# A linear-attention, gated-MLP and mixture-of-experts kernel: a first activation placed ahead, and fewer unread matmuls

## The chip, the cores and the metric

The kernel runs on one core of a Trainium2 chip. The metric is the device time of one execution in microseconds, as the median of several runs. The core's engines work side by side and meet at semaphores: TensorE (PE) multiplies matrices, VectorE (DVE) and ScalarE (ACT) do elementwise work, GpSimd (POOL) does fills, some elementwise work and indexed transfers, and SyncE (SP) issues the other transfers. Each engine takes its instructions in order.

## The reference, cut to what matters

```python
# 1. linear attention: batch 4, 8 heads, 768 tokens, head size 48
f = 1.0 / (1.0 + np.exp(-f_logit))
for t in range(S):
    state = f[:, :, t, :, None] * state + np.einsum('bhd,bhe->bhde', k[:, :, t], v[:, :, t])
    y[:, :, t] = np.einsum('bhd,bhde->bhe', q[:, :, t], state)
# 2. gated MLP on 3072 tokens x 384, with 1536 hidden columns; x is y with its heads side by side
gate = 1.0 / (1.0 + np.exp(-(x @ w_gate)))
x = gate * (x @ w_val) @ w_out
# 3. top-1 mixture of 8 experts with 1024 hidden columns
expert_idx = np.argmax(x @ w_gate2, axis=1)          # its softmax weight is gate_w
out[i] = gate_w[i] * (np.maximum(x[i] @ w1[e], 0) @ w2[e])   # e = expert_idx[i], if it has room
```

The weights of part 2 arrive in 64 bits per number and are turned into 32-bit numbers on the chip.

## The kernel before, in words

The 3072 tokens are 24 tiles of 128. The first six tiles (SPLIT_FROM) go through attention in one form, the later ones in another; only the first form bears on the change. Its stages for tile i are: s0a transposes the forget logits on TensorE (line 372) and takes Tanh of half of them on ScalarE (line 386); s0b makes the decay of it (Identity, line 397), a sum for a range check (Exp, line 399) and a running product over the tokens by a scan on VectorE (line 405, result ck); s0c takes a reciprocal (414) and a second scan (416, result cq); s1 transposes k and q on TensorE (441, 443); s1b multiplies them by ck and cq on VectorE (458, results kt and qt); s3 transposes kt back (509); s2 makes the scores (482) and s2b masks them on VectorE (501); s4 makes the state (542); s5 the output (626); s6 transposes it (647) for the MLP.

Beside it the 36 pieces of the MLP's weights are converted, one piece per call of weights_step: three bit operations on VectorE (784, 792, 799) make 32-bit numbers, ScalarE (866) and VectorE (867) split them into a high and a low part. For a piece of w_out TensorE also transposes it (862), ScalarE copies that (873), and TensorE multiplies it by the gate of part 3 (884), whose result VectorE splits (891, 892).

From about 48 us the MLP runs over 8 blocks of three tiles: line 904 makes gate and value, lines 914 to 922 combine them, line 937 multiplies by w_out. Attention of later tiles and conversion of later pieces run between its matmuls. The experts follow from line 1295 on.

The string EARLY (lines 29 to 35) lists the stages of the first tiles and the conversions (W) ahead of the MLP. Between them stand calls of pace: it issues matmuls of a constant tile, pace_in, whose result no instruction reads, and keeps them in program order. PACE has three numbers: how many stand at the very start, how many right behind the first transposes of tile 0, and how many behind each W and each stage that uses TensorE. The list has 34 places of the last kind, so PACE = (7, 12, 2) makes 7 + 12 + 68 = 87.

Within the kernel's text a scheduler orders the instructions of TensorE, VectorE, ScalarE and GpSimd by its own estimates of when their inputs are ready; SyncE's queue keeps the order of the text (manual_schedule). So a change in a few instructions can move others. The first loads are issued in the order of the string LOADS: the forget logits of tile 0, then k and q of tile 0 (k0), a piece of raw weights (r0), the logits of tile 1 (f1), and so on; q of tile 1 is the second transfer of k1.

```python
LOADS = "k0 r0 f1 r1 v0 k1 r2 r3 v1"
PACE = (7, 12, 2)
```

```python
            if i == 0:
                pace(PACE[1])
```

```python
            if item == "W":
                weights_step()
                pace(PACE[2])
```

Of the kernel before, what the change touches and what calls it, by code (L numbers as in the profile page):

```python
# [14 lines left out]
AF = mybir.ActivationFunctionType  # L15
# [36 lines left out]

PIECE = 192

PACE = (7, 12, 2)

DECAY_ON_POOL = 6
X_MIN = -80.0
# [12 lines left out]
def kernel(  # L71
# [15 lines left out]
    nc = tc.nc  # L87
# [69 lines left out]
    def by_head(t):  # L157
        return t.rearrange("p (h d) -> p h d", h=H)
# [56 lines left out]
    z_all = const.tile([P, NTILE], F32, name="z_all")  # L215
    tiny = const.tile([P, 2], F32, name="tiny")
# [4 lines left out]
    def select(t, fill, pattern, base, cmul, op=ALU.is_ge):  # L221
        nc.gpsimd.affine_select(
            out=t, in_=t, pattern=pattern, compare_op=op, fill=fill, base=base, channel_multiplier=cmul
        )

    def make_constants():
        nc.gpsimd.memset(ident, 0.0)
        select(ident, 1.0, [[-1, P]], 0, 1, ALU.not_equal)
        for t, pad in ((xf_r, X_PAD), (xq_r, 0.0), (xk_r, 0.0)):
            for z in range(2):  # L230
                nc.gpsimd.memset(by_head(t[:, z])[:, :, D:], pad)
        nc.gpsimd.memset(decay[:, ::PS], 0.0)
        nc.gpsimd.memset(lim, DECAY_CLAMP)
        nc.gpsimd.memset(flush[:, 0:1], 512.0)
        nc.gpsimd.memset(flush[:, 1:2], -512.0)
        nc.gpsimd.memset(one, 1.0)
        nc.gpsimd.memset(tiny[:, 0:1], -(2.0**-15))
        nc.gpsimd.memset(tiny[:, 1:2], 2.0**-15)
        nc.gpsimd.memset(below, 0.0)
        nc.gpsimd.memset(half, 0.5)  # L240
        nc.gpsimd.memset(mask, 1.0)
        select(mask, 0.0, [[1, P]], 0, -1)
        for z in range(2):
            r = slice(HT * z, HT * z + HT)
            nc.gpsimd.tensor_copy(hmask[r], mask[r, r])
        nc.gpsimd.memset(e_all, 1.0)

        nc.gpsimd.memset(umask, 1.0)
        select(umask[:, 0:D], 0.0, [[0, D]], D - 1, -1)
        select(umask[:, D:], 0.0, [[0, D]], -64, 1)  # L250
        select(umask[:, D:], 0.0, [[0, D]], 64 + D - 1, -1)
# [69 lines left out]
    def pace(n):  # L321
        for _ in range(n):
            ins = nc.tensor.matmul(pace_out, lhsT=pace_in[:, 0:P], rhs=pace_in, start=True, stop=True)  # L323
            tc.keep_in_program_order(ins)
# [43 lines left out]
    def s0a(i):  # L368
        if i < SPLIT_FROM:
# [3 lines left out]
            if i == 0:  # L373
                pace(PACE[1])
        else:
# [1010 lines left out]
    with tc.manual_schedule(engines={mybir.EngineType.SP}):  # L1386
        load_f(0)
        nc.vector.memset(pace_in, 1.0)
        pace(PACE[0])
        make_constants()  # L1390
        nc.sync.dma_start(out=wg2, in_=moe2_w_gate.rearrange("(k p) e -> p k e", p=P))
        for what in LOADS.split():
            {"f": load_f, "k": load_qk, "v": load_v, "r": load_raw}[what[0]](int(what[1:]))
# [3 lines left out]
        def weights_step():  # L1397
            n = next_split[0]
            for lag, fn in (
                (2, split3),  # L1400
                (0, convert1),
                (1, split2),
                (0, convert2),
                (0, convert3),
                (1, split2b),
            ):
                if 0 <= n - lag < NU:
                    fn(order[n - lag])
            next_split[0] += 1
# [49 lines left out]
        for item in EARLY.split():  # L1459
# [3 lines that stand above are left out]
            else:  # L1463
                i, stage = item.split(".")
                stages[stage](int(i))
                if stage in ("s0a", "s1", "s2", "s3", "s4", "s5", "s6"):
                    pace(PACE[2])
        started[0] = True
# [375 lines left out]
```

## Time and profile before

| | us |
|---|---|
| median of 3 runs | 860.74 (860.14 to 861.27) |
| profiled execution | 860.37 |
| its span, first to last instruction | 858.6 |

| engine | busy us | share of the span |
|---|---|---|
| TensorE | 838.5 | 98% |
| VectorE | 541.7 | 63% |
| ScalarE | 396.5 | 46% |
| GpSimd | 160.7 | 19% |

Busy time counts the lengths of an engine's instructions without counting a moment twice. An instruction often starts while the one before it is still ending, so what one costs in a row of its like is the distance of their starts, which is a little less than its length. [...]

### The profile page before, as it was taken

The page shows a single profiled execution, that of the slowest core. Times are in us where ns is not written, and L with a number is a line of the kernel's source. Part 1 is how long each engine was busy: PE and PEld are TensorE (multiplying, and loading weights), DVE is VectorE, ACT ScalarE, POOL GpSimd, SP SyncE. Part 2 cuts the span into 40 slices and gives each one's busy share as a digit, 9 for nine tenths or more (in the row PEclk, how much of TensorE's full clock was granted, in tenths as well). Part 3 has the DMA queues.
Part 4 walks back from the last instruction along what each step waited for, and adds up shares of the span by engine and source line. Part 5 has one row for each costly group of instructions (what it writes and reads, how often), then busy time and mean ns, then how long its engine had stood idle before and what let it go on. Part 6 is the DMA issues. An engine that isn't in the chain of part 4 may idle for free.

```text
span 858.6 us, 18219 instructions
## 1 busy us (share of the span) xinstructions
PE 838.5 (98%) x7042; PEld 791.4 (92%) x7042; DVE 541.7 (63%) x1300; ACT 396.5 (46%) x1011; POOL 160.7 (19%) x240
## 2 busy tenths in 40 slices
PE   8999999999999999999999999999899999999995
PEld 5789989999999999999999999999899999999994
DVE  6998988767766766866866763552953544553521
ACT  3543433555455555555555544332642533553421
POOL 2031200001011011110011000110563524432311
PEclk9999999999999999999999999999999999999998
DMA  9955443544653643644444532140665325434000
GB/s 203 208 153 146 140 118 103 116 116 114 147 116 89 170 108 90 168 101 107 130 107 99 134 85 59 47 166 1 206 229 171 134 88 189 163 100 134 27 23 26
DMA packets 137746, 103.74 MB, mean 121 GB/s; under 512 B 66456, under 2 KB 130760, under 8 KB 137650
## 3 DMA queue, kind: packets, MB, share of 16 engines
q1 hardware_dynamic: 134034, 93.04, 40.7%
q0 software_dynamic: 3616, 9.44, 3.3%
q8 instruction: 57, 0.93, 0.5%
q14 instruction: 39, 0.32, 0.1%
HBM read 89.95 MB, written 13.46 MB: 120 GB/s over the span
## 4 chain that ended last, share of the span: by engine, by line
PE 79%; DVE 8%; issue 6%; ACT 3%; DMA 2%; POOL 1%; SPq 0%; POOLq 0%; ACTq 0%; DVEq 0%
PE pg L904 16%; PE acc L937 16%; PE pv L904 16%; PE acc L1316 6%; PE pg L1295 5%; PE pv L1295 5%; PE acc L1331 2%; PE a L681 1%; PE a L525 1%; PE a L470 1%; DMA x<-xt 1%; PE a L1274 1%; PE acc L323 1%; POOL out_dram L1373 1%; PE a L1331 1%
## 5 line engine op out<-in xcount | busy, mean ns | idle before, releaser
L916 DVE SCALAR_TENSOR_TENSOR th<-th,pv 128x384 f32<-128x384 f32 x96 | 52.9, 551 | 86.7 <-PE pv L904 85.5
L904 PE MATMUL pg<-xh,wh 128*128 128x384 f32 x288 | 102.5, 356 | 1.4 <-ACT th L914 1.2
L937 PE MATMUL acc<-oh,hh 128*128 128x392 f32 x288 | 100.5, 349 | 0.0
L937 PE MATMUL acc<-ol,hh 128*128 128x392 f32 x288 | 98.5, 342 | 0.0
L937 PE MATMUL acc<-oh,hl 128*128 128x392 f32 x288 | 98.3, 341 | 0.0
L904 PE MATMUL pg<-xl,wh 128*128 128x384 f32 x288 | 97.2, 337 | 0.3 <-DVE xl L734 0.3
L904 PE MATMUL pg<-xh,wl 128*128 128x384 f32 x288 | 96.8, 336 | 0.0
L904 PE MATMUL pv<-xh,wh 128*128 128x384 f32 x288 | 96.5, 335 | 0.3 <-DVE th L916 0.3
L904 PE MATMUL pv<-xl,wh 128*128 128x384 f32 x288 | 96.6, 335 | 0.0
L904 PE MATMUL pv<-xh,wl 128*128 128x384 f32 x288 | 96.5, 335 | 0.0
L914 ACT ACTIVATE th<-pg 128x384 f32<-128x384 f32 x96 | 46.9, 488 | 99.8 <-PE pg L904 98.3
L921 ACT CAST hh<-th 128x384 fp32r<-128x384 f32 x96 | 49.2, 512 | 87.4 <-DVE th L916 87.4
L922 DVE TENSOR_TENSOR hl<-th,hh 128x384 fp32r<-128x384 f32 x96 | 53.3, 555 | 33.2 <-ACT hh L921 32.7
L821 ACT ACTIVATE piece<-piece,tiny 128x192 f32<-128x192 f32 x144 | 67.1, 467 | 7.0 <-DMA piece<-in_moe_w_out_dram 2.3
L904 PEld LDWEIGHTS pg<-xh,wh 128*128 128x128 f32 x288 | 54.1, 188 | 5.1 <-ACT th L914 2.0
L904 PEld LDWEIGHTS pg<-xl,wh 128*128 128x128 f32 x288 | 54.2, 188 | 0.8 <-DVE xl L734 0.8
L904 PEld LDWEIGHTS pv<-xh,wh 128*128 128x128 f32 x288 | 54.1, 188 | 0.6 <-DVE th L916 0.6
L937 PEld LDWEIGHTS acc<-oh,hh 128*128 128x128 f32 x288 | 54.0, 188 | 0.6
L937 PEld LDWEIGHTS acc<-oh,hl 128*128 128x128 f32 x288 | 54.1, 188 | 0.2
L904 PEld LDWEIGHTS pg<-xh,wl 128*128 128x128 f32 x288 | 54.1, 188 | 0.1
L937 PEld LDWEIGHTS acc<-ol,hh 128*128 128x128 f32 x288 | 54.2, 188 | 0.0
L904 PEld LDWEIGHTS pv<-xl,wh 128*128 128x128 f32 x288 | 54.1, 188 | 0.0
(341 smaller groups left out, 2014.7 us busy)
## 6 DMA issues: line engine op xcount, KB each, us to landing
r<-in_moe_w_dram SPq DMA_DIRECT2D x16, 1536.0 KB, 7.8
raw<-in_moe_w_out_dram SPq DMA_DIRECT2D x12, 384.0 KB, 4.2
raw<-in_moe_w_gate_dram SPq DMA_DIRECT2D x12, 384.0 KB, 3.6
v<-in_v_dram SPq DMA_DIRECT2D x24, 192.0 KB, 3.3
raw<-in_moe_w_val_dram SPq DMA_DIRECT2D x12, 384.0 KB, 3.4
x1d<-x SPq DMA_DIRECT2D x24, 192.0 KB, 1.9
piece<-in_moe_w_gate_dram SPq DMA_DIRECT2D x24, 192.0 KB, 3.6
piece<-in_moe_w_val_dram SPq DMA_DIRECT2D x24, 192.0 KB, 3.4
```

The costliest lines, as they stand in the source:

```text
L323: ins = nc.tensor.matmul(pace_out, lhsT=pace_in[:, 0:P], rhs=pace_in, start=True, stop=True)
L470: nc.tensor.matmul(sc[z][t, p * HT : (p + 1) * HT], lhsT=pair(kt, p)[64 * z : 64 * z + D, t], rhs=pair(qt, p)[64 * z : 64 * z + D, t], sta ...
L821: nc.scalar.activation(out=words[:, :, 0], in_=words[:, :, 1], func=AF.Sign, bias=tiny[:, z : z + 1], accum_out=above[:, z, n % NF : n % N ...
L904: nc.tensor.matmul(ps[:, 0:nt], lhsT=w[:, kk, :], rhs=x[:, kk, 0:nt], start=(m == 0), stop=(m == len(ops) - 1))
L914: nc.scalar.activation(out=th[:, 0:nt], in_=pg[:, 0:nt], func=AF.Tanh, scale=0.5)
L916: nc.vector.scalar_tensor_tensor(out=g[:, 0:nt], in0=th[:, 0:nt], scalar=1.0, in1=pv[:, 0:nt], op0=ALU.add, op1=ALU.mult)
L921: nc.scalar.copy(out=hh[:, 0:nt], in_=g[:, 0:nt])
L922: nc.vector.tensor_tensor(out=hl[:, 0:nt], in0=g[:, 0:nt], in1=hh[:, 0:nt], op=ALU.subtract)
L937: nc.tensor.matmul(acc[i][:, 0:DE], lhsT=a[:, ts], rhs=w, start=(f == 0 and m == 0), stop=(f == NF - 1 and m == 2),)
L1295: nc.tensor.matmul(ps, lhsT=wt[:, kk, fs], rhs=x[:, kk, c0 : c0 + w], start=(m == 0), stop=(m == len(ops) - 1))
L1316: nc.tensor.matmul(acc[e, d][:, 0 : CAPS[e]], lhsT=w[:, f, d * P : (d + 1) * P], rhs=a[:, 0 : CAPS[e]], start=(f == 0 and m == 0), stop=(f ...
L1331: nc.tensor.matmul(acc[e, j][0:n, 0:DM], lhsT=a[:, ss], rhs=w[:, f], start=(f == 0 and m == 0), stop=(f == NF2 - 1 and m == 2),)
```

## The change

Two places are edited. The middle and last numbers of PACE are halved. And behind make_constants, which fills the constants on GpSimd, a Tanh of one column is added on ScalarE: it reads the constant tiny and writes the first column of z_all, a column that the sum of tile 0 (line 399) overwrites later. Lines behind 1390 move down by one.

```diff
--- before.py
+++ after.py
@@ -52,7 +52,7 @@
 
 PIECE = 192
 
-PACE = (7, 12, 2)
+PACE = (7, 6, 1)
 
 DECAY_ON_POOL = 6
 X_MIN = -80.0
@@ -1388,6 +1388,7 @@
         nc.vector.memset(pace_in, 1.0)
         pace(PACE[0])
         make_constants()
+        nc.scalar.activation(out=z_all[:, 0:1], in_=tiny[:, 0:1], func=AF.Tanh)
         nc.sync.dma_start(out=wg2, in_=moe2_w_gate.rearrange("(k p) e -> p k e", p=P))
         for what in LOADS.split():
             {"f": load_f, "k": load_qk, "v": load_v, "r": load_raw}[what[0]](int(what[1:]))
```

SyncE's and GpSimd's orders stay as they were. TensorE's, VectorE's and ScalarE's differ up to about 95 us and agree from there on. A number behind a name is a buffer's.

ScalarE, before, its first instructions (decay is the Tanh of tile 0's logits, a_183 the logits transposed):

```order
L386 ACT_TABLE_LOAD [waits PE_49]
L386 ACTIVATE decay<-a_183 128x4x128 [waits Pool_49]
L397 ACTIVATE decay<-decay,bias 128x4x128 [waits Activation_49,Pool_49]
L399 ACTIVATE a_183,z_all<-a_183 128x512
L386 ACTIVATE decay<-pv 128x4x128 [waits DVE_49,PE_49,Activation_49]
```

And after (a_184 is the same tile as a_183):

```order
L1391 ACT_TABLE_LOAD
L1391 ACTIVATE z_all<-tiny 128x1 [waits Pool_49]
L386 ACTIVATE decay<-a_184 128x4x128 [waits PE_49]
L397 ACTIVATE decay<-decay,bias 128x4x128 [waits Activation_49,Pool_49]
L399 ACTIVATE a_184,z_all<-a_184 128x512
L386 ACTIVATE decay<-pv 128x4x128 [waits DVE_49,PE_49,Activation_49]
```

The table load stands first now, with no wait, and the new instruction behind it waits for GpSimd. The rows behind are as they were but for kn, the copy of line 511, which comes earlier.

TensorE, before, from the transposes of kt of tile 0 (a_251) to its scores (a_260, a_261):

```order
L509 MATMUL a_251<-ident,kt 128x112 [waits DVE_49]
L509 MATMUL a_251<-ident,kt 128x112 x3
L323 LDWEIGHTS pace_in
L323 MATMUL acc_124<-pace_in 128x512
L323 LDWEIGHTS pace_in
L323 MATMUL acc_124<-pace_in 128x512
L482 MATMUL a_260<-qt,kt 128x128 [waits DVE_49,Activation_49]
L482 MATMUL a_261<-qt,kt 128x128 [waits PE_49]
L482 MATMUL a_260<-qt,kt 128x128
```

And after, from the transposes of kt (a_242) to the scores (a_250, a_251); acc_278 is q of tile 1:

```order
L509 MATMUL a_242<-ident,kt 128x112 [waits DVE_49]
L509 MATMUL a_242<-ident,kt 128x112 x3
L323 LDWEIGHTS pace_in
L323 MATMUL acc_124<-pace_in 128x512
L443 MATMUL acc_278<-ident,xq 128x128 [waits DMAHW1_49,PE_49]
L443 MATMUL acc_278<-ident,xq 128x128 x2
L482 MATMUL a_250<-qt,kt 128x128 [waits DVE_49,Activation_49]
L482 MATMUL a_251<-qt,kt 128x128 [waits PE_49]
L482 MATMUL a_250<-qt,kt 128x128
```

One filler stands in place of two at each place, and three of the four transposes of tile 1's q, which wait for a load (DMAHW1), have come in front of the scores.

VectorE, before, from the second scan of tile 1 to the split of the first w_out piece's last columns (oh_274; a_337 and a_339 are the masked scores of tile 0, kt and qt are tile 1's):

```order
L416 SCALAR_TENSOR_TENSOR cq<-decay,lim 128x516
L867 TENSOR_TENSOR ol_275<-a,oh_274 128x384
L867 TENSOR_TENSOR wl_326<-a,wh_325 128x384
L501 TENSOR_TENSOR a_337<-a_260,mask 128x512
L784 TENSOR_SCALAR a<-raw 128x384
L501 TENSOR_TENSOR a_339<-a_261,mask 128x512
L792 SCALAR_TENSOR_TENSOR a<-raw,a 128x384
L458 TENSOR_TENSOR kt<-pv,ck 128x512
L799 SCALAR_TENSOR_TENSOR a<-raw,a 128x384
L891 CAST oh_274<-acc_317 128x8
L458 TENSOR_TENSOR qt<-acc_290,cq 128x512
L892 TENSOR_TENSOR ol_275<-acc_317,oh_274 128x8
```

And after, from the first bit operation on the third piece to the products of tile 1 (oh_263 is the same tile as oh_274):

```order
L784 TENSOR_SCALAR a<-raw 128x384
L416 SCALAR_TENSOR_TENSOR cq<-decay,lim 128x516
L867 TENSOR_TENSOR wl_312<-a,wh_311 128x384
L891 CAST oh_263<-acc_303 128x8
L792 SCALAR_TENSOR_TENSOR a<-raw,a 128x384
L892 TENSOR_TENSOR ol_264<-acc_303,oh_263 128x8
L799 SCALAR_TENSOR_TENSOR a<-raw,a 128x384
L501 TENSOR_TENSOR a_322<-a_250,mask 128x512
L501 TENSOR_TENSOR a_324<-a_251,mask 128x512
L458 TENSOR_TENSOR kt<-pv,ck 128x512
L458 TENSOR_TENSOR qt<-acc_278,cq 128x512
```

The split of line 891 has come forward: the two masked scores, the product kt, and the bit operations 792 and 799 of the third piece stand behind it now.

## Rows read from the trace of the kernel before

**Rows 1.** The page: busy time of each engine, then the chain that ended last by engine

```profile
PE 838.5 (98%) x7042; PEld 791.4 (92%) x7042; DVE 541.7 (63%) x1300; ACT 396.5 (46%) x1011; POOL 160.7 (19%) x240
...
PE 79%; DVE 8%; issue 6%; ACT 3%; DMA 2%; POOL 1%; SPq 0%; POOLq 0%; ACTq 0%; DVEq 0%
```

**Rows 2.** Busy us (instructions) of PE, PEld, DVE, ACT, POOL; clock, DMA share, GB/s

```profile
5.35:48.20 42.85, 41.38 (x337) 29.93 (x336) 38.54 (x86) 21.58 (x46) 4.75 (x13) 1.00 1.02 217
...
10.00:24.00 14.00, 12.88 (x116) 9.39 (x115) 13.93 (x30) 5.58 (x13) 0.19 (x1) 1.00 1.00 211
...
34.00:52.40 18.40, 18.29 (x140) 14.04 (x137) 17.31 (x41) 8.72 (x19) 6.83 (x16) 1.00 0.93 203
...
140.00:848.00 708.00, 704.17 (x6079) 675.98 (x6077) 421.75 (x1038) 336.36 (x887) 134.22 (x154) 1.00 0.41 115
```

**Rows 3.** ScalarE in order of time: start, length, line, operation, [idle before]

```profile
5.64 1.28 ACT L386 ACT_TABLE_LOAD   x1 [5.64 <-PE a L372]
6.93 0.60 ACT L386 ACTIVATE decay<-a 128x512 f32<-128x512 f32 x1
7.62 0.72 ACT L397 ACTIVATE decay<-decay,bias 128x512 f32<-128x512 f32 x1
```

**Rows 4.** VectorE in order of time, the same columns

```profile
8.38 1.23 DVE L405 TENSOR_TENSOR_SCAN ck<-decay,lim 128x516 f32<-128x516 f32 x1 [5.52 <-ACT decay L397]
...
20.09 0.69 DVE L458 TENSOR_TENSOR kt<-pv,ck 128x512 f32<-128x512 f32 x1
20.69 0.55 DVE L799 SCALAR_TENSOR_TENSOR a<-raw,a 128x384 uint32<-128x384 uint32 x1
21.16 0.16 DVE L891 CAST oh<-acc 128x8 fp32r<-128x8 f32 x1
...
41.78 0.56 DVE L867 TENSOR_TENSOR ol<-a,oh 128x384 fp32r<-128x384 f32 x1 [0.39 <-ACT oh L866]
...
42.52 0.17 DVE L891 CAST oh<-acc 128x8 fp32r<-128x8 f32 x1 [0.17 <-PE acc L884]
...
47.18 0.17 DVE L891 CAST oh<-acc 128x8 fp32r<-128x8 f32 x1 [0.41 <-PE acc L884]
```

**Rows 5.** TensorE in order of time, the same columns

```profile
1.53 3.17 PE L323 MATMUL acc<-pace_in 128*128 128x512 bf16 x7 [1.53 <-DVE pace_in L1388]
...
5.35 3.23 PE L323 MATMUL acc<-pace_in 128*128 128x512 bf16 x14
...
10.59 0.59 PE L323 MATMUL acc<-pace_in 128*128 128x512 bf16 x2
...
12.28 0.60 PE L509 MATMUL a<-ident,kt 112*128 112x112 f32 x4 [1.10 <-DVE kt L458]
...
13.25 1.16 PE L482 MATMUL a<-qt,kt 48*128 48x128 f32 x16
...
14.79 0.49 PE L862 MATMUL pg<-ident,a 128*128 128x128 f32 x3
...
15.54 0.60 PE L441 MATMUL pv<-ident,xk 128*128 128x128 f32 x4
...
16.94 0.67 PE L542 MATMUL a<-v,kn 128*64 128x48 f32 x16
...
17.98 0.73 PE L884 MATMUL acc<-wg,wot 128*128 128x8 f32 x6
```

**Rows 6.** SyncE's queue: the load of the second tile's q

```profile
8.05 1.85 SPq L287 DMA_DIRECT2D xq<-in_q_dram  x1
```

**Rows 7.** Transfers issued from 8.0 to 8.5: KB each, us to landing

```profile
xq<-in_q_dram SPq DMA_DIRECT2D x1, 192.0 KB, 5.3
```

**Rows 8.** The matmuls of line 323: ns min/median/max, first and last start

```profile
L323 PE MATMUL acc<-pace_in x87: 376/379/634, 1.5 to 48.0; 128*128 128x512 bf16 x87
```

**Rows 9.** TensorE's last matmul

```profile
847.76 0.34 PE L1331 MATMUL acc<-w2h,hl 128*112 128x384 f32 x1
```

**Rows 10.** Busy time by stretch at the end, columns as in group 2

```profile
852.00:852.50 0.50, 0.00 (x0) 0.00 (x0) 0.00 (x0) 0.00 (x0) 0.00 (x0) 0.50 0.20 29
```

## The prediction

> **What bounds the kernel now.** I read the page first, then busy time by stretch, the engines' rows in order of time for the first 50 us, the landing times, and the end of the span. TensorE is busy for 98% of the span and has 79% of the chain of waits [rows 1]. From 140 to 848 us it is busy for 704.17 of 708.00 us [rows 2]. There is next to no idle time in which to win back or lose anything, so whatever lead the start hands over at about 140 us reaches the end unchanged. The change lies in the first 48 us only, and there the picture differs. Of TensorE's time in that stretch a large part is the filler of line 323, whose results nobody reads: 87 matmuls in all, the last at 48.0 us [rows 8]. What is full there is VectorE: 13.93 of 14.00 us from 10 to 24 us and 17.31 of 18.40 from 34 to 52.4 us [rows 2]. So the start is a race of two full engines, and only one of them is full of work that must be done. The head of it is one chain: filler, four transposes of tile 0's forget logits, ScalarE's table load of 1.28 us, Tanh at 6.93 us, the Identity at 7.62 us [rows 3], and VectorE's first scan at 8.38 us, after 5.52 us of waiting [rows 4].
>
> **The table load.** In the order before, the load carries the wait for the transposes; after, it stands first on ScalarE with no wait, and the one-column Tanh behind it waits for POOL alone. ScalarE is idle for its first 5.64 us [rows 3], so both fit ahead of the transposes. Tanh can then start at 5.64 instead of 6.93 us: 1.28 us off the head, and VectorE's first scan moves from 8.38 to 7.10 us. The added instruction costs nothing, as ScalarE has nothing else then; were POOL's constant later than the transposes, the gain would shrink by that lateness. Bounds: 0 to 1.28 us, taken as 1.28. [...]
>
> **The filler.** A filler matmul costs (3.23 - 0.59) / 12 = 0.22 us on TensorE at the full clock: 14 of them last 3.23 us and 2 of them 0.59 us [rows 5]. Of 87, 7 + 6 + 34 x 1 = 47 stay, so 40 go: 40 x 0.22 = 8.8 us of TensorE's time. If TensorE were the bound throughout, all 8.8 us would be won; if VectorE were, nothing. VectorE's rows are the nearer: from 10 to 24 us it is idle for only 0.07 us, so there nothing can be won behind the head. From 34 to 52.4 us it is idle for 1.09 us, of which three waits make 0.39 + 0.17 + 0.41 = 0.97 us. Two are for line 884 on TensorE and one is for ScalarE's copy, which stands in the same queue of conversions [rows 4]. With half the filler TensorE gets to line 884 earlier, and I count these 0.97 us as won (bounds 0 and 1.09).
>
> **What the new order costs.** The scheduler moves the real work too, and SyncE's queue is unmoved. After, TensorE has three transposes of the second tile's q (line 443) in front of the scores of the first tile (line 482). That q is issued at 8.05 us [rows 6] and lands 5.3 us later [rows 7], at 13.35 us, and no change makes it earlier: its issue waits for no engine. TensorE's queue is in order, so the scores, line 862, line 542 and line 884 wait behind it. Before, line 482 started at 13.25 and line 884 at 17.98 us, 4.73 us apart, with 8 fillers and four line-443 transposes between [rows 5]. After, 4 fillers (0.88 us) and three transposes (0.45 us, at 0.60 for four by line 441) are gone from between, and the three stand in front: 13.35 + 0.45 + 4.73 - 0.88 - 0.45 = 17.20 us, and line 884 ends 0.73 us later, at 17.93 us.
>
> VectorE needs that result for line 891. Before, line 891 came 21.16 - 8.38 = 12.78 us after the first scan, all of it dense. After, five of the instructions stand behind it instead of in front: two of line 501, one kt product (0.60 us from start to start; the mask products of the same size taken like it), one of line 792 and one of line 799 (0.47 us, the one taken like the other) [rows 4]. They are 3 x 0.60 + 2 x 0.47 = 2.74 us. VectorE is there at 7.10 + 12.78 - 2.74 = 17.14 us and waits until 17.93: a new wait of 0.79 us that eats over half of the head start. The same line comes a second time, near 29 us, early in the new order, behind a cut-up line 626. Its wait lies between 0 and 0.79 us; I take 0.30, nearer to 0, since by then the loads come sooner too.
>
> **Sum.** 1.28 - 0.79 - 0.30 + 0.97 = 1.16 us. The profiled execution took 860.37 us (858.6 of span and 1.8 around it), so it would take 859.21. It lies 0.37 us under the median of the runs, 860.74, so the median would be 859.58, said as 859.6. A measurement of this kernel can tell about 0.2%, 1.7 us, from no change; so the forecast is a small gain that counts as none.
>
> **Rivals.** *The new waits don't come.* If q lands earlier, or VectorE is later than my sum, both new waits vanish: 1.28 + 0.97 = 2.25 us, 858.5; with every idle moment of VectorE up to 52.4 us gone it is 2.4 us, 858.3, and more only if later waits go too. For it: VectorE was never idle from 10 to 24 us, whatever TensorE did. Against it: the landing is a row, and TensorE's order is fixed.
>
> *The clock falls in the new gap; slower.* After, kt is ready no sooner than 7.10 + 1.23 + 0.69 = 9.02 us (scan and product [rows 4], with the short reciprocal between them left out), line 509 lasts 0.60, one filler 0.22, and TensorE then has nothing from 9.84 until 13.35: up to 3.5 us idle, where before the longest gap near there was 1.10 us [rows 5], at a granted clock of 1.00 all through [rows 2]. [...] If the clock falls, TensorE's work from 13.35 to 17.93 us, 4.58 us, doubles at worst, and VectorE waits for it: 1.28 - (0.79 + 4.58) - 0.30 + 0.97 = -3.42, 864.2. If the clock is back after half of that work, it is -1.13, 861.9. I take the middle, 863.0. It decides once more than 1.16 us is lost to the half clock. Against it: at the front 7 fillers run at half speed, in 3.17 us, and the 14 behind them in 3.23 us [rows 5], so the clock came back soon once TensorE was kept busy.
>
> *The clock stays down until the dense matmuls.* It may be the filler that holds the full clock between the small matmuls and transposes of the start, and half of it may not do. TensorE is busy for 41.38 us from 5.35 to 48.20 us [rows 2], of which 80 x 0.22 = 17.6 are filler and 23.8 the rest. With 40 fillers, 8.8 us, it is 32.6 us, at half clock 65.2, or 22 us more than the 42.85 us of that stretch: about 883. [...]
>
> *The change doesn't do what it says*: hardly, as the order shows the load ahead and 40 fillers gone.
>
> **How the numbers follow.** Forecast 0.46, 859.6 with its own range 858.4 to 860.9. No new waits 0.27, 858.5, reaching to 857.2. Clock falls in the gap 0.21, 863.0, from 861.7 to 864.2. Clock stays down 0.04, 883. The rest, 0.02, slower. Faster by over 0.2% means below 859.0: 0.08 of the forecast's share and 0.25 of the second, 0.33. Slower means above 862.5: 0.15 of the third, with the last two, 0.21. Within 0.2% is the rest, 0.46. The range 857.3 to 863.6 leaves out a little of the second case below, and above it the worst of the third and all of the fourth.
>
> **What would show it.** Tanh of tile 0 at 5.6 us and the first scan at 7.1 (table load). TensorE idle from about 10 to 13.4 us with line 443 behind it, and VectorE waiting 0.8 us for line 884 ahead of its first line 891 near 17 to 18 us (new wait). No waits of VectorE for line 884 near the old 42.5 and 47.2 us (filler). A granted clock of 1.00 from 10 to 48 us (no rival three or four). From 140 us on every row should stand earlier by one and the same amount, the gain. I am wrong if that amount is over 1.7 us, if the clock falls, or if the stretches from 52 to 140 us, where the order also differs a little, change it by more than 1 us.

## The result, and the profile after

The changed kernel takes 870.23 us (median, 868.42 to 870.81), and the kernel before took 860.44 us (859.94 to 861.27) beside it: a ratio of 1.0113 [1.01, 1.0127], or 9.8 us slower. The forecast was 859.6 us in a range of 857.3 to 863.6, with a chance of 0.21 for slower. It was wrong in sign, and the miss of 10.6 us is nine times its sum of 1.16. The profiled execution took 870.42 us, with a span of 868.7.

The busy times of the page hardly differ from those of [rows 1]: TensorE has 1.7 us more in spite of 40 fewer matmuls, and its share of the chain rose from 79 to 84%.

```profile
PE 840.2 (97%) x7002; PEld 795.2 (92%) x7002; DVE 542.8 (62%) x1300; ACT 396.8 (46%) x1012; POOL 160.2 (18%) x240
...
PE 84%; issue 5%; DVE 4%; ACT 2%; DMA 2%; POOL 1%; SPq 1%; POOLq 0%; DVEq 0%; ACTq 0%
```

Busy time by stretch, in the columns of [rows 2], with the clock ahead of the last two:

```profile
5.00:11.00 6.00, 4.36 (x28) 2.61 (x26) 4.41 (x9) 3.09 (x7) 0.80 (x16) 1.00 1.15 239
11.50:18.00 6.50, 4.43 (x25) 3.46 (x26) 3.24 (x8) 1.31 (x4) 0.43 (x1) 0.50 1.20 262
18.50:24.50 6.00, 4.79 (x49) 3.84 (x47) 5.20 (x12) 2.60 (x7) 0.00 (x0) 1.00 0.59 151
25.00:31.50 6.50, 6.50 (x45) 4.41 (x43) 4.82 (x10) 2.17 (x6) 0.19 (x1) 0.50 0.97 175
32.00:38.00 6.00, 5.00 (x42) 4.48 (x41) 4.23 (x13) 1.77 (x4) 0.00 (x0) 1.00 0.22 56
39.00:45.00 6.00, 5.90 (x30) 4.19 (x31) 4.88 (x12) 1.82 (x4) 0.00 (x0) 0.50 0.75 158
46.00:59.00 13.00, 10.69 (x87) 8.91 (x87) 11.94 (x28) 5.92 (x14) 6.66 (x16) 1.00 0.71 174
59.50:62.00 2.50, 2.50 (x10) 2.40 (x9) 1.72 (x6) 0.84 (x2) 0.00 (x0) 0.50 0.49 105
63.00:848.00 785.00, 778.81 (x6610) 746.32 (x6609) 495.34 (x1198) 370.43 (x957) 144.86 (x169) 1.00 0.42 118
```

The clock, TensorE's granted one as a share of full speed, which [rows 2] show at 1.00 throughout, falls to 0.50 four times before 63 us and not again until the end. By the records of the clock the four falls last 23.9 us together. The row from 25.0 to 31.5 us also shows why busy time misleads: TensorE is "busy" all of it, with 45 matmuls at a clock of 0.50. And VectorE, full in [rows 2], has holes now: 3.24 of 6.50, 4.82 of 6.50, 4.88 of 6.00.

ScalarE's head, answering [rows 3] (start, length, line, operation, [idle before]):

```profile
0.81 1.28 ACT L1391 ACT_TABLE_LOAD   x1 [0.81 <-PEq L1827]
2.91 0.20 ACT L1391 ACTIVATE z_all<-tiny 128x1 f32<-128x1 f32 x1 [0.81 <-POOL tiny L237]
5.11 0.60 ACT L386 ACTIVATE decay<-a 128x512 f32<-128x512 f32 x1 [2.00 <-PE a L372]
```

Then VectorE, answering [rows 4]:

```profile
6.56 1.23 DVE L405 TENSOR_TENSOR_SCAN ck<-decay,lim 128x516 f32<-128x516 f32 x1 [3.69 <-ACT decay L397]
...
17.67 0.36 DVE L784 TENSOR_SCALAR a<-raw 128x384 uint32<-128x384 uint32 x1 [3.26 <-PE pg L862]
...
20.42 0.17 DVE L891 CAST oh<-acc 128x8 fp32r<-128x8 f32 x1 [0.80 <-PE acc L884]
...
27.94 0.69 DVE L501 TENSOR_TENSOR a<-acc,mask 128x512 f32<-128x512 f32 x1 [1.47 <-PE pv L482]
...
32.28 0.17 DVE L891 CAST oh<-acc 128x8 fp32r<-128x8 f32 x1 [1.00 <-PE acc L884]
...
35.21 0.17 DVE L891 CAST oh<-acc 128x8 fp32r<-128x8 f32 x1 [1.38 <-PE acc L884]
...
43.64 0.69 DVE L501 TENSOR_TENSOR a<-a,mask 128x512 f32<-128x512 f32 x1 [1.12 <-PE a L482]
...
47.96 0.56 DVE L867 TENSOR_TENSOR ol<-a,oh 128x384 fp32r<-128x384 f32 x1 [0.82 <-ACT oh L866]
...
49.99 0.16 DVE L891 CAST oh<-acc 128x8 fp32r<-128x8 f32 x1
...
55.00 0.15 DVE L891 CAST oh<-acc 128x8 fp32r<-128x8 f32 x1
```

And TensorE, answering [rows 5] and [rows 9]:

```profile
9.98 0.38 PE L323 MATMUL acc<-pace_in 128*128 128x512 bf16 x1
13.57 0.88 PE L443 MATMUL acc<-ident,xq 128*128 128x128 f32 x3 [3.21 <-DMA xq<-in_q_dram]
14.37 2.08 PE L482 MATMUL a<-qt,kt 48*128 48x128 f32 x16
...
16.79 0.85 PE L862 MATMUL pg<-ident,a 128*128 128x128 f32 x3
...
19.65 0.73 PE L884 MATMUL acc<-wg,wot 128*128 128x8 f32 x6
...
54.36 0.44 PE L904 MATMUL pg<-xh,wh 128*128 128x384 f32 x1
...
57.57 0.44 PE L904 MATMUL pg<-xl,wh 128*128 128x384 f32 x1 [2.15 <-DVE xl L657]
...
857.36 0.34 PE L1331 MATMUL acc<-w2h,hl 128*112 128x384 f32 x1
```

The first scan starts 1.82 us earlier (8.38 to 6.56). TensorE then stands still for 3.21 us until q lands, and the clock falls in that time, at 11.3 us. The sixteen scores take 2.08 us where they took 1.16, and VectorE waits 3.26 us for line 862. The last matmul ends up 9.60 us later (847.76 to 857.36). The loss is made at the start. Before, the first line 904 was this:

```profile
48.48 0.44 PE L904 MATMUL pg<-xh,wh 128*128 128x384 f32 x1
```

It comes 5.88 us later now, and the tenth matmul of its name 9.95 us later (68.29 to 78.24). Between these two TensorE took 19.8 us before and takes 23.9 now. In this stretch lie the wait of 2.15 us for line 657 on VectorE, where TensorE waited 0.28 us at most before, and the last fall of the clock. The first matmul of the experts whose rows are x2h, line 1295, comes 9.5 us later (639.7 to 649.2). TensorE, at full clock from 63 us on, carries the loss to the end.

### The profile page after: what moved, and what is told of

It is laid out like the page before. It is cut to its first block, busy times and chain, and to the rows that moved or that the text cites. A ratio compares the mean times of both kernels' runs of the same rounds, so it can differ in the third digit from the quotient of the medians.

```text
span 868.7 us, 18142 instructions
## 1 busy us (share of the span) xinstructions
PE 840.2 (97%) x7002; PEld 795.2 (92%) x7002; DVE 542.8 (62%) x1300; ACT 396.8 (46%) x1012; POOL 160.2 (18%) x240
## 4 chain that ended last, share of the span: by engine, by line
PE 84%; issue 5%; DVE 4%; ACT 2%; DMA 2%; POOL 1%; SPq 1%; POOLq 0%; DVEq 0%; ACTq 0%
PE pg L904 17%; PE acc L937 17%; PE pv L904 17%; PE acc L1316 6%; PE pg L1295 5%; PE pv L1295 5%; PE acc L1331 2%; PE a L681 1%; PE a L525 1%; PE a L1274 1%; PE a L470 1%; POOL out_dram L1373 1%; PE a L1331 1%; PE a L626 1%; PE a L509 1%
## 5 line engine op out<-in xcount | busy, mean ns | idle before, releaser
L922 DVE TENSOR_TENSOR hl<-th,hh 128x384 fp32r<-128x384 f32 x96 | 53.3, 555 | 32.1 <-ACT hh L921 31.5
L904 PEld LDWEIGHTS pv<-xh,wl 128*128 128x128 f32 x288 | 54.5, 189 | 0.0
```

The costliest lines, as they stand in the source:

```text
L904: nc.tensor.matmul(ps[:, 0:nt], lhsT=w[:, kk, :], rhs=x[:, kk, 0:nt], start=(m == 0), stop=(m == len(ops) - 1))
L922: nc.vector.tensor_tensor(out=hl[:, 0:nt], in0=g[:, 0:nt], in1=hh[:, 0:nt], op=ALU.subtract)
```

## The experiments

Each edit is told against the changed kernel, whose PACE is (7, 6, 1). "A", "B" and the like are as the expectation in question defines them. The times of before beside them are 860.31 us for the first four, 860.41 for the next four and 859.64 for the last three. "Half clock" is the time at 0.50 ahead of 800 us in the profiled execution, by the records of the clock. That execution is the fastest of its four for "thin late" (863.84 us), and one of 861.96 us for "middle halved".

| run | PACE, fillers | median us (runs) | ratio to before | half clock us |
|---|---|---|---|---|
| load only | (7, 12, 2), 87 | 859.35 (12) | 0.9986 [0.9975, 0.9996] | 0 |
| filler only | (7, 6, 1), 47 | 869.83 (4) | 1.0100 [1.0073, 1.0127] | 27.3 |
| last halved | (7, 12, 1), 53 | 868.76 (6) | 1.0077 [1.0051, 1.0103] | 23.9 |
| middle halved | (7, 6, 2), 81 | 863.28 (11) | 1.0036 [1.0014, 1.0058] | 3.4 |
| last at 3 | (7, 12, 3), 121 | 862.61 (9) | 1.0026 [1.0015, 1.0037] | 0 |
| middle at 18 | (7, 18, 2), 93 | 859.08 (12) | 0.9983 [0.9974, 0.9992] | 0 |
| gap filled | (7, 6, 1) + 15, 62 | 860.60 (10) | 0.9997 [0.9985, 1.0009] | 6.8 |
| no filler | (7, 0, 0), 7 | 877.74 (4) | 1.0192 [1.0173, 1.0211] | 58.0 |
| early hole | 7, 12, 0 then 2, 73 | 865.80 (4) | 1.0069 [1.0052, 1.0086] | 10.2 |
| q sooner | (7, 6, 1), 47 | 869.90 (4) | 1.0121 [1.0104, 1.0138] | 20.5 |
| thin late | 7, 12, 2 then 1, 60 | 866.12 (4) | 1.0073 [1.0056, 1.0090] | 10.2 |

Where the number of fillers changes, the scheduler mostly moves real work too. Leaving out the fillers, TensorE's order is one and the same in before, "load only" and "middle at 18"; in the changed kernel and "q sooner"; and in "gap filled" and "thin late". VectorE's order differs in places in each of these groups too.

### The two parts apart

```diff
-PACE = (7, 6, 1)
+PACE = (7, 12, 2)
```

> The early Tanh alone, with all 87 fillers (PACE 7, 12, 2); TensorE's order is that of before. Theory A (the half clock in four stretches between 11 and 63 us, which the thinner filler lets in, costs the 10 us, and the table load is a gain of its own): clock 1.00 from 5 us on, first scan of VectorE 1.3 us earlier (7.1 us or sooner), time 1.0 to 1.5 us under before, about 859.2. Rival B (the load was hidden anyway, or its lead is lost to VectorE later): 860.4 within 0.4.

It measured 859.35 us, 0.96 us under before. VectorE's first scan, and the clock over nearly all of the span:

```profile
7.04 1.23 DVE L405 TENSOR_TENSOR_SCAN ck<-decay,lim 128x516 f32<-128x516 f32 x1 [4.18 <-ACT decay L397]
```

```profile
6.00:848.00 842.00, 833.71 (x7024) 789.26 (x7028) 540.84 (x1298) 394.18 (x1010) 154.90 (x190) 1.00 0.45 122
```

The scan comes 1.34 us earlier than in [rows 4] and about 1 us of that reaches the end. This half of the change does what the prediction said.

```diff
-        nc.scalar.activation(out=z_all[:, 0:1], in_=tiny[:, 0:1], func=AF.Tanh)
```

> The halved filler alone (PACE 7, 6, 1), without the early Tanh. Theory A: the clock falls as in the changed kernel and the 1.3 us of the table load are missing as well, so about 11 us over before, 871.5 (870 to 873). Rival B (the early Tanh, by moving the head, is what makes TensorE idle for 3.2 us before the load of q lands): the gap is shorter by 1.3 us, the clock holds, and the time is within 2 us of before.

It measured 869.83 us, just under the range that A gave, with falls at about 11.6, 25.3, 35.5 and 59.4 us. TensorE still waits for q, for 2.57 us. The loss belongs to the filler, with the order that came with it, all of it. The early Tanh saves nothing beside it: the changed kernel, which has both, is 9.8 us over before, and this one 9.5.

### Which number of PACE, and which direction

```diff
-PACE = (7, 6, 1)
+PACE = (7, 12, 1)
```

> Early Tanh, and only the last number of PACE halved (7, 12, 1): 53 fillers. The scheduler now leaves the transposes of tile 1's q (line 443) behind the scores, so that TensorE does not stop for the load of q. Theory A1 (each thin stretch drops the clock by itself): several stretches at half clock, 866 to 870. Rival A2 (it is the one gap of 3.2 us ahead of line 443 that starts it, and the later falls follow from the first): clock 1.00 throughout, 858 to 860.

868.76 us. In this order q's transposes stand behind the scores again, and no wait for their load is left. The clock holds through the first 20 us and falls after it, at 20.4, 34.0 and 68.2 us:

```profile
5.00:20.00 15.00, 12.98 (x102) 9.07 (x101) 12.84 (x26) 7.14 (x16) 1.21 (x16) 1.00 1.20 250
20.50:27.00 6.50, 6.28 (x33) 4.73 (x34) 4.06 (x12) 2.02 (x5) 0.00 (x0) 0.50 1.15 233
27.50:34.00 6.50, 5.88 (x61) 5.51 (x58) 4.89 (x13) 2.10 (x5) 0.19 (x1) 1.00 0.31 76
34.50:47.50 13.00, 11.58 (x57) 8.17 (x60) 8.97 (x22) 4.91 (x11) 0.00 (x0) 0.50 0.86 179
```

TensorE's longest waits before the first fall are these two (start, length, operation, [idle before]):

```profile
17.77 0.63 PE L372 MATMUL a<-ident,xf 128*128 128x128 f32 x4 [0.73 <-DMA xf<-in_f_logit_dram]
19.40 2.36 PE L626 MATMUL a<-v,a 128*128 128x48 f32 x14 [1.00 <-DVE a L501]
```

So a wait of 3 us isn't needed for the clock to fall; [rows 5] have one of 1.10 us, and there the clock held.

```diff
-PACE = (7, 6, 1)
+PACE = (7, 6, 2)
```

> Early Tanh, and only the middle number halved (7, 6, 2): 81 fillers, six fewer right behind the first transposes. Theory A: TensorE is idle somewhat longer between 7 and 10 us, all later stages keep their two fillers, so the clock holds and the time is that of the early Tanh alone, about 859.2 (858.5 to 860). Rival C (it is the middle number that matters, since the first fall comes at 11 us): a fall at about 11 us and 863 or more.

863.28 us, and the widest spread of all: from 860.91 us in a run with a mean clock of 0.993 to 868.79 us in one with 0.986. The program was the same each time, so the time goes with the clock where the order can't differ. The kernel before has a little of this too: of its 24 runs beside this one, 17 lay under 861.0 us, at 0.995 to 0.997, and the six slowest (861.61 to 863.76) at 0.991 to 0.994. A straight line through the times and clocks of the eleven runs here gives 858.6 us at 0.996, the clock of most runs of the load alone, and one through the six of "last halved" 858.9. By this estimate the two kernels would be no slower than the load alone if their clock held.

The median lies in the range of rival C, but the fall doesn't lie where C has it. The one fall of the profiled execution comes at 20.9 us:

```profile
21.00:24.00 3.00, 2.89 (x13) 1.82 (x14) 2.90 (x8) 1.88 (x4) 0.00 (x0) 0.50 1.08 190
```

```diff
-PACE = (7, 6, 1)
+PACE = (7, 12, 3)
```

> Early Tanh, and the last number raised (7, 12, 3): 121 fillers, 34 more than before, some 7.5 us more of TensorE's time in the first 48 us. Theory A (filler is worth its TensorE time while VectorE is the full engine, and more of it holds the clock more surely): clock 1.00 in every run, 859 to 861. Rival D (87 fillers leave TensorE no slack, so more of them go straight onto the path): 3 to 7 us over the early Tanh alone, 862 to 866, at a clock of 1.00.

862.61 us with no fall, as rival D gave. More filler than before, with the order that it brings, costs 3.3 us over the load alone: 34 matmuls, about 0.10 us each.

```diff
-PACE = (7, 6, 1)
+PACE = (7, 18, 2)
```

> Early Tanh, and the middle number raised (7, 18, 2): 93 fillers. Theory A: no fall of the clock, and the six more run while VectorE has its first scan, so 859.3 as with the early Tanh alone (858.8 to 860.3). Rival D: six more cost 6 x 0.22 = 1.3 us at the head, since the transposes of k stand behind them, 860.6.

859.08 us, the fastest version tried. Its interval doesn't part it from the load alone, whose median is 0.27 us higher.

### Where the filler stands

```diff
-                    pace(PACE[2])
+                    pace(PACE[2] + (15 if item == "0.s3" else 0))
```

> The changed kernel with 15 more fillers in one place, behind the transposes of tile 0's kt (line 509), where it stood idle for 3.21 us: 62 fillers; q's transposes go back behind the scores. Theory A1 (each thin stretch drops the clock by itself): no fall at 11 us, but falls from 20 us on as in the kernel with only the last number halved, 866 to 870. Rival A2 (the first fall sets off the others): clock 1.00 throughout, 858.5 to 861.

860.60 us, in the range of A2, though the clock doesn't hold throughout. With 15 fillers behind line 509 the scheduler put q's transposes behind the scores, so the gap went in two ways at once. The profiled execution has two short falls in place of four:

```profile
5.00:32.00 27.00, 24.73 (x211) 18.65 (x213) 24.78 (x54) 12.72 (x29) 1.74 (x18) 1.00 1.08 230
32.50:35.00 2.50, 2.50 (x17) 1.79 (x17) 2.42 (x7) 0.90 (x2) 0.00 (x0) 0.50 0.80 209
36.00:49.00 13.00, 10.63 (x87) 8.46 (x86) 11.95 (x29) 6.74 (x15) 5.56 (x15) 1.00 0.89 185
49.50:52.00 2.50, 2.50 (x9) 2.50 (x9) 2.50 (x7) 0.58 (x2) 0.70 (x2) 0.50 0.84 224
```

62 fillers do better here than 81 in the run "middle halved", so the number of them doesn't decide. And its four fastest runs (858.76 to 859.78 us, mean clock 0.994 to 0.995) are no faster than the load alone (858.51 to 860.06), which has 25 fillers more: where the clock nearly holds, leaving those out wins nothing.

```diff
-PACE = (7, 6, 1)
+PACE = (7, 0, 0)
```

> Early Tanh, and no filler behind the first seven (7, 0, 0). Theory A: half clock for most of the time until the MLP's matmuls are dense (about 55 us), yet TensorE is also free of 47 x 0.22 = 10 us of filler; the stretch is as bad as or worse than with half the filler, 868 to 880. Rival E (the halved filler is the worst of both, and without any TensorE has so much room that half the clock is enough for VectorE): 864 or less.

877.74 us, as theory A gave. The clock is at 0.50 for most of the time up to 67 us. From 67 to 77 us, where the MLP's matmuls follow each other and TensorE is busy for 10.00 of 10.00 us, it is 1.00, and it falls twice more for a short time, at 77 and 91 us:

```profile
9.00:19.00 10.00, 7.16 (x51) 6.08 (x51) 6.06 (x13) 3.69 (x9) 0.43 (x1) 0.50 1.26 244
...
22.50:49.50 27.00, 22.78 (x126) 20.53 (x127) 18.69 (x42) 7.80 (x19) 0.19 (x1) 0.50 0.53 118
...
53.50:66.50 13.00, 12.71 (x62) 11.62 (x62) 11.39 (x25) 2.99 (x7) 7.18 (x16) 0.50 0.63 161
67.00:77.00 10.00, 10.00 (x67) 8.98 (x66) 7.46 (x20) 5.27 (x12) 0.00 (x0) 1.00 0.40 111
```

### One gap, or thin stretches

Two theories were left: the gap ahead of q's transposes brings the first fall and this the later ones, or each thin stretch falls by itself. First the gap is taken away, with the order on TensorE and the 47 fillers as they are:

```diff
-LOADS = "k0 r0 f1 r1 v0 k1 r2 r3 v1"
+LOADS = "k0 r0 f1 k1 r1 v0 r2 r3 v1"
```

> The changed kernel with k and q of tile 1 loaded ahead of the second raw piece and of v of tile 0: TensorE's order is that of the changed kernel, 47 fillers, but line 443 finds its q about 2 to 3 us earlier, so its wait of 3.21 us falls to under 1.5 us. Theory B (that one wait sets off the falls): no fall at 11 us and few later, 860 to 863 us. Theory A (the thin filler loses the clock by itself, as with 53 fillers and no wait for a load): the first fall moves to about 18 to 25 us and the later ones stay, 866 to 870 us; v of tile 0 comes later and can delay the output of tile 0 by up to 1 us.

869.90 us: no gain. Yet the edit did what it was to do. TensorE waits for q for 0.91 us in place of 3.21, and the longest wait up to 20 us is 1.07 us:

```profile
11.34 0.52 PE L443 MATMUL acc<-ident,xq 128*128 128x128 f32 x3 [0.91 <-DMA xq<-in_q_dram]
...
17.89 0.63 PE L372 MATMUL a<-ident,xf 128*128 128x128 f32 x4 [1.07 <-DMA xf<-in_f_logit_dram]
19.55 0.42 PE L626 MATMUL a<-v,a 128*128 128x48 f32 x2 [1.03 <-DVE a L501]
```

The clock holds to 20.3 us, and then its first fall is longer than any in the changed kernel:

```profile
7.00:20.00 13.00, 9.55 (x84) 6.78 (x82) 11.99 (x24) 5.97 (x15) 0.62 (x2) 1.00 1.23 247
20.50:30.50 10.00, 9.78 (x59) 7.71 (x61) 6.56 (x14) 2.73 (x8) 0.19 (x1) 0.50 0.84 176
```

So the one gap isn't the cause of the loss. Then two parts of the start are thinned apart, each against the full filler and with the load ahead. The early part is left with no filler, where the changed kernel has one at each place:

```diff
-PACE = (7, 6, 1)
+PACE = (7, 12, 2)
+HOLE = range(0, 11)
-        for item in EARLY.split():
+        for at_, item in enumerate(EARLY.split()):
+            few = 0 if at_ in HOLE else PACE[2]
```

(Both calls of pace behind these lines take few.)

> 73 fillers: 7 at the start, 12 behind the first transposes, none at the seven places up to the second conversion (line 441 to line 482 of tile 0), two at each of the 27 places behind. Three of the four transposes of tile 1's q stand in front of the first scores, as in the changed kernel, so TensorE waits for their load again at about 11 to 13.5 us. Theory A (each thin stretch loses the clock by itself): one fall, at 11 to 13 us, none or a short one later, since the later filler is as in the kernel before; some 7 us at half clock at 0.38 us each, 859.4 + 2.7 = 862 us (861 to 864). Theory B (the first fall brings the later ones, since the late attention stages and the filler do not catch up): falls again at about 25, 38 and 58 us as in the changed kernel, 866 to 870 us.

865.80 us, over what theory A gave and just under what B gave. There are three short falls, near 14, 24 and 65 us, 10.2 us in all; the wait for q is 2.19 us here. The second lies where two fillers stand at each place as before. So falls can come with an early hole and full filler behind it, though not the whole series of them. And the clock is not all of its loss: the four runs took 865.36 to 866.46 us at a mean clock of 0.990, where the four runs of "last halved", "middle halved" and "thin late" with that clock took 863.20 to 864.40. The wait for q may be the rest; no run shows it.

The late part, told against the edit just shown:

```diff
-            few = 0 if at_ in HOLE else PACE[2]
+            few = 2 if at_ in FULL else PACE[2]
```

(Here PACE is (7, 12, 1), and FULL names the same eleven items.)

> 60 fillers: as before up to the second conversion (7, 12, and two at each of the first seven places), one at each of the 27 places behind. No wait for q's load in front of the scores. Theory B (falls come from a first fall in the early gap): the clock holds throughout, 859 to 860.5 us. Theory A (thin stretches by themselves): falls from about 25 us on, where only one filler stands at a place, two or three of them, 864 to 868 us.

866.12 us, as theory A gave. Nothing falls in the full stretch, and two falls lie in the thin one:

```profile
5.00:32.00 27.00, 23.94 (x205) 18.03 (x206) 23.97 (x52) 12.35 (x28) 1.27 (x17) 1.00 1.08 229
32.50:38.50 6.00, 5.70 (x29) 4.22 (x31) 4.88 (x12) 1.82 (x4) 0.00 (x0) 0.50 0.90 163
39.00:52.50 13.50, 11.13 (x91) 9.38 (x90) 11.90 (x28) 6.25 (x14) 6.62 (x16) 1.00 0.72 165
53.00:56.00 3.00, 3.00 (x12) 2.91 (x11) 2.23 (x7) 0.87 (x2) 0.00 (x0) 0.50 0.68 159
```

The first line 904 comes at 47.90 us here, 0.58 us earlier than before and 0.49 later than in the load alone. So the long fall had cost little up to there. This execution loses its time behind it, in a stretch with a wait of 2.15 us for VectorE like that of the changed kernel and with the second fall.

Over before, the early hole costs 6.2 us, the thin late part 6.5, and the changed kernel 9.8. But a thin late part doesn't decide by itself. "Gap filled" has the same single filler at each of these 27 places and the same order of TensorE's real work, with 62 fillers against 60, and it took 860.60 us. The two differ in the fillers up to the second conversion and in the orders of VectorE and ScalarE.

## Why the prediction was wrong

**The step that failed** is the rival "the clock falls in the new gap", its price and its place among the cases. It was seen, with its gap (up to 3.5 us foretold, 3.21 measured) and with the landing of q (13.35 foretold; line 443 starts at 13.57). But it was priced as one fall that is over once line 884 is done, 861.7 to 864.2 us, and it was given 0.21, because "the clock came back soon once TensorE was kept busy". The clock does come back, at 18.1 us. But the filler is half as thick from there on and the clock falls again, three times. The rival next to it, in which the filler holds the clock, was nearer in kind, with 0.04 and an estimate of 883 us: 0 us were at half clock with the 87 fillers of the load alone, 58.0 with 7. The truth lies between the two: many falls, each of which ends. In the sum itself the half clock stands at nothing; 23.9 us of it were measured. That the filler, with the order that it brings, makes the change slower is shown by "filler only"; that the half clock is what costs the time, by the runs of one program, whose order can't differ and whose time goes with their clock ("middle halved": 860.91 us at 0.993, 868.79 at 0.986).

**The size** can be worked out from the runs. The profiled execution less the 859.35 us of the load alone, divided by the time at half clock, is 11.1 / 23.9 = 0.46 for the changed kernel, 0.48 for "q sooner", 0.44 for "thin late", 0.41 for "last halved", 0.63 for "early hole" and 18.7 / 58.0 = 0.32 for no filler. Small amounts scatter more (0.24 and 0.77). Each share takes in whatever else the order of its run changed. In the changed kernel three fillers in a row start 0.43 us apart at half clock (from 39.9 us) and seven 0.22 us apart at the full one (from 4.9 us), so by this estimate TensorE loses at most about half of the time at half clock, and the 0.63 of "early hole" has something else in it. By the others a microsecond at half clock cost a third to a half of one. The prediction counted 4.58 us of work that doubles at worst, which isn't far off for one fall; there were four.

**The filler's term.** 40 matmuls went, as foretold, and 8.8 us of TensorE's time with them, but the 0.97 us counted as won don't show in any time. "Gap filled" is no faster than the load alone where its clock nearly holds, and 6 more fillers behind the first transposes cost nothing either (859.08); three per place did cost. Of the waits that this term was to remove, the two for line 884 are gone: they stood ahead of the fifth and sixth line 891 (42.52 and 47.18 us before), which start at 49.99 and 55.00 us now without a wait, but late. The wait for ScalarE's copy grew from 0.39 to 0.82 us, and new waits for line 884, 1.00 and 1.38 us, came ahead of the second and third line 891.

**The waits of the new order.** At the first line 891 0.79 us was foretold and 0.80 measured, but that is chance. The prediction's sum had VectorE dense up to there, and it was not. It stood for 3.26 us at line 784, which waits for line 862. Line 784 writes a tile of two buffers for the third piece, line 862 reads the buffer that it needs, and line 862 stands behind q's transposes. The order in the section on the change shows line 784 moved in front of line 416; the sum followed results alone and not the buffer's reader. The second wait, taken as 0.30, was 1.00; the work ahead of it ran at half clock up to 31.7 us.

**The table load** was right: 1.28 us foretold at the head, 1.34 measured in the scan of the load alone, and 0.96 us at the end. The changed kernel's scan came 1.82 us earlier. Fewer fillers aren't the reason: "q sooner" has the same 47, and its scan starts at 7.04 us as in the load alone. The difference lies in the first rise of the clock, at 4.4 us in the profiled execution of the changed kernel and at 6.6 and 5.9 us in these two: the four transposes ahead of Tanh took 0.60 us there and 1.06 us here.

**Of what was to show it**, Tanh came at 5.11 (5.6 foretold) and the scan at 6.56 (7.1); TensorE was idle from 10.4 to 13.57; the clock was not 1.00 from 10 to 48 us, which the prediction named as what would make it wrong. The late rows do stand off by nearly one amount, 9.5 us at the first line 1295 of x2h and 9.60 at the last matmul, but later and not earlier; at 142 us it was 10.7. And the stretch from 52 to 140 us did change the lead by more than 1 us, which the prediction named as well: the lag is 5.88 us at the first line 904 and 9.95 at the tenth.

**Still open**: what exactly makes the clock fall at one place and not at another. No run thins the filler and keeps the order of all engines, so how much of the falls comes from fewer fillers and how much from the order that the scheduler makes of them isn't shown; "gap filled" and "thin late" are 5.5 us apart with one order on TensorE. The early hole has a second fall where the filler is full, and no run separates a shifted order of the later work from an after-effect of the first fall. The full version loses a little of the clock itself in some runs, as the spread of before's own runs shows (a mean clock of 0.991 to 0.997).

## What to carry to other kernels

Work whose results nobody reads can still matter to the clock: here the kernel with 7 fillers was at half clock for 58.0 us ahead of 800, the same one with 87 for none. Before thinning it, ask what the granted clock does without it in each stretch, and price a fall as often as a thin stretch comes, not once; then try half of it by place, since where it stands counted for more here than how much there is (62 fillers took 860.60 us, 81 took 863.28), and compare the orders before you put a difference down to the filler. When a queue moves, follow for each moved instruction not only who reads its result but also whose buffer it hands back.

## What the runs showed of the hardware

The clock fell with no wait of TensorE over 1.07 us ahead of it ("q sooner", with 9.55 of 13.00 us busy from 7 to 20 us), while the kernel before held it across a wait of 1.10 us [rows 5], with TensorE busy for 12.88 of 14.00 us around it [rows 2]. Longer waits do stand ahead of the last falls: in the changed kernel, "q sooner", "gap filled" and "thin late" one of about 2.15 us of line 904 ends 0.4 to 1.5 us ahead of the fall, but in "last halved" one of 1.90 us, which ends at 56.2 us, has no fall behind it until 68.2. So the longest gap alone didn't tell the falls in advance. And fillers cost less than their length: 6 more than the 87 cost nothing ("middle at 18"), and 34 more ("last at 3", whose order differs too) 0.10 us each, where TensorE spends 0.22 us on one.
